# Aligned buffers, the norm's deviation moved into the residual addition, and a new order of operations

## The chip, the cores and the metric

The kernel runs on one core of a Trainium2 chip. The metric is the device time of one execution in microseconds (us). A core has five engines that run their own instruction queues side by side: TensorE (PE; its weight loads are shown as PEld), VectorE (DVE), ScalarE (ACT), GpSimd (POOL) and SyncE (SP), which issues the loads and stores here. They wait for each other by semaphores.

## What is computed

Three layers, one behind the other, in float32, on 2 batches of 768 positions and 512 channels (8 heads of 64).

```python
# 1. attention: each query sees keys within 16 positions, and 24 block summaries (max of k, mean of v)
scores = concat(where(|i - j| < 16, q k^T / 8, -1e9), q k_sum^T / 8 + log(32))
x = softmax(scores) @ concat(v, v_sum)
# 2. a gated MLP with a 3-tap convolution over positions
h = max(x @ w_in, 0)                      # 512 -> 1024
x = (h * sigmoid(conv3(h, conv_w))) @ w_out
# 3. layer norm, feed-forward, residual
xn = (x - mean(x)) / sqrt(var(x) + 1e-6) * g_ln
out = x + max(xn @ w_ch1, 0) @ w_ch2      # 512 -> 2048 -> 512
```

## The kernel before

Products that need more than one pass split an operand into a high part (rounded to fp32r) and a low part (the rest), and sum three matmuls (high x high, high x low, low x high).

Attention works on 12 blocks of 128 positions: transposes of k and q (L374, L367), scores (L479 mask, L487), softmax on VectorE, ScalarE and GpSimd, transposes of the probabilities (L586) and the product with v (L503). The MLP works on 5 groups of 2 or 3 blocks; in each it goes over 8 hidden blocks (`m_step`, numbers 0 to 39): the product with w_in (L741), relu on ScalarE (L753), three taps (L771), tanh (L776), the gate on VectorE (L786), its high part (L265/L267) and low part (L804), and the product with w_out (L818). The result, x, is copied out of PSUM by ScalarE with a row sum (L827), and a second pass gives the sum of squares (L834).

The feed-forward part goes over 16 steps; step n takes a batch b and a slice i of the hidden channels, in the order (0,0), (0,1), (1,0), (1,1), (1,2), (1,3), (0,2), (0,3) and so on. A step has seven products of six matmuls each (L1288, `pr`), a Strassen-like scheme whose sums are made by VectorE (L1299), high and low parts of the relu (L1308, L1311), and six accumulations of six matmuls (L1366, `ac`). PSUM has two banks for the products, so a product waits for the sum that frees the bank of the one before last. After the last step of a run of steps of one batch the accumulated result is added to x (L1375, L1357 at the very end) and, at the end, stored.

The norm, before: from the squares `ln_stats` makes the variance on VectorE (L1068), its power of -1/2 on GpSimd (L1071, `rs`) and mean times deviation (L1073, `nb`). Then `x_ops` normalizes each block (`xn`, L1191 on ScalarE, L1194 on VectorE), TensorE transposes it (L1229, `tp`), and it is split into high and low parts. g_ln is multiplied into w_ch1.

What stands where on an engine is set by a table, `ORDER`: some 1,930 words like `31P`, the number of an operation and the letter of the engine that runs it. The kernel records each operation with the engines that it may use, and issues them in the order of the table; each engine takes its own in that order and waits where an operand is not ready.

Buffers lie on two sides of SBUF: `const`, then `x2a` and `x2b`, then the pool `m1` (weights wi and wo, the gate's buffers) and later `m2` in its place, from the left; `at` and later `p2` from the right.

## Time and profile before

| | us |
|---|---|
| median of 3 runs (lowest, highest) | 474.7 (474.35, 474.94) |
| the profiled execution | 474.33 |
| its span, first to last instruction | 472.6 |

| engine | busy us | share of the span |
|---|---|---|
| TensorE (PE) | 462.8 | 98% |
| its weight loads (PEld) | 407.4 | 86% |
| VectorE | 351.3 | 74% |
| ScalarE | 249.4 | 53% |
| GpSimd | 142.0 | 30% |

The profiled execution's time is its span and 1.7 us around it. Times in a timeline count from the span's start. A matmul's duration covers more than the step from it to the next one, since matmuls are pipelined; start minus start tells what a stretch of them takes.

### The profile page before, as it was taken

The page shows a single profiled execution, that of the slowest core. Times are in us where ns is not written, and L with a number is a line of the kernel's source. Part 1 is how long each engine was busy: PE and PEld are TensorE (multiplying, and loading weights), DVE is VectorE, ACT ScalarE, POOL GpSimd, SP SyncE. Part 2 cuts the span into 40 slices and gives each one's busy share as a digit, 9 for nine tenths or more (in the row PEclk, how much of TensorE's full clock was granted, in tenths as well). Part 3 has the DMA queues.
Part 4 walks back from the last instruction along what each step waited for, and adds up shares of the span by engine and source line. Part 5 has one row for each costly group of instructions (what it writes and reads, how often), then busy time and mean ns, then how long its engine had stood idle before and what let it go on. Part 6 is the DMA issues. An engine that isn't in the chain of part 4 may idle for free.

```text
span 472.6 us, 8644 instructions
## 1 busy us (share of the span) xinstructions
PE 462.8 (98%) x3211; PEld 407.4 (86%) x3211; DVE 351.3 (74%) x705; ACT 249.4 (53%) x654; POOL 142.0 (30%) x185
## 2 busy tenths in 40 slices
PE   6999999999999999999999999999999999999997
PEld 5658999888899989988989899989898898998985
DVE  2899999996777857998999874677655677654643
ACT  2788999666766666958953532232343235322010
POOL 3537432554125244231513321131131331002000
PEclk9999999999999999999999999999999999999999
DMA  8999975902002202002221041201222022110213
GB/s 244 328 245 216 248 213 147 177 3 63 1 18 47 92 2 89 1 0 90 90 90 56 33 135 58 77 23 67 89 90 89 2 89 84 46 50 1 96 39 133
DMA packets 56121, 43.26 MB, mean 92 GB/s; under 512 B 34404, under 2 KB 46976, under 8 KB 56080
## 3 DMA queue, kind: packets, MB, share of 16 engines
q1 hardware_dynamic: 55936, 42.65, 32.2%
q8 instruction: 25, 0.41, 0.4%
q14 instruction: 16, 0.13, 0.1%
q10 hardware_dynamic: 144, 0.07, 0.1%
HBM read 39.22 MB, written 3.15 MB: 90 GB/s over the span
## 4 chain that ended last, share of the span: by engine, by line
PE 89%; DMA 4%; DVE 2%; SPq 2%; issue 1%; ACT 1%; POOL 1%; ACTq 0%; POOLq 0%
PE acc L1366 26%; PE ch L1288 23%; PE x L818 12%; PE h L741 6%; PE tr L741 5%; PE ch L741 4%; PE h L818 2%; PE tr L503 2%; PE tr L487 2%; PE tr L586 2%; DMA vw<-in_v_dram 2%; DMA raw<-in_moe_w_ch_dram 1%; DMA early<-in_q_dram 1%; PE acc L1229 1%; PE tr L367 1%; PE tr L479 1%
## 5 line engine op out<-in xcount | busy, mean ns | idle before, releaser
L1366 PE MATMUL acc<-w,cb 128*128 128x512 f32 x570 | 139.0, 391 | 0.0
L1366 PEld LDWEIGHTS acc<-w,cb 128*128 128x128 f32 x570 | 106.3, 188 | 19.2
L1288 PE MATMUL ch<-xb,w 128*128 128x384 f32 x384 | 75.6, 338 | 0.3 <-DVE u L1299 0.3
L1288 PEld LDWEIGHTS ch<-xb,w 128*128 128x128 f32 x384 | 68.0, 188 | 3.4 <-DVE u L1299 1.1
L1299 DVE TENSOR_TENSOR u<-ch,u 128x384 f32<-128x384 f32 x64 | 35.0, 553 | 31.1 <-PE ch L1288 30.5
L1288 PE MATMUL ch<-xt,w 128*128 128x384 f32 x288 | 56.9, 337 | 0.3 <-DVE u L1299 0.2
L771 DVE SCALAR_TENSOR_TENSOR c<-h,ccol,c 128x256 f32<-128x256 f32 (+1 forms) x80 | 48.2, 613 | 9.6 <-POOL c L269 4.9
L1288 PEld LDWEIGHTS ch<-xt,w 128*128 128x128 f32 x288 | 51.0, 188 | 2.9 <-DVE u L1299 0.9
L818 PE MATMUL x<-wo,ghi 128*128 128x512 f32 x160 | 51.5, 403 | 0.0
L1099 POOL TENSOR_TENSOR w<-raw,w 128x512 fp32r<-128x512 f32 (+1 forms) x16 | 20.5, 1282 | 82.4 <-ACT w L1166 75.4
L1308 ACT ACTIVATE cb<-p 128x384 fp32r<-128x384 f32 x32 | 16.6, 521 | 40.9 <-PE acc L1366 23.8
L557 ACT ACTIVATE prob<-tr,nm 128x120 f32<-128x120 f32 x96 | 33.2, 367 | 5.9 <-DVE nm L545 3.9
L647 ACT ACTIVATE raw<-raw 128x512 f32<-128x512 f32 x32 | 21.0, 674 | 26.2 <-DMA raw<-in_moe_w_ch_dram 24.6
L741 PE MATMUL h<-xT,wi 128*128 128x258 f32 x216 | 31.9, 288 | 0.0
L818 PE MATMUL x<-wo,glo 128*128 128x512 f32 x80 | 31.6, 394 | 0.0
L818 PEld LDWEIGHTS x<-wo,ghi 128*128 128x128 f32 x160 | 27.9, 189 | 3.4 <-ACT wo L265 0.2
L1308 ACT ACTIVATE cb<-u 128x384 fp32r<-128x384 f32 x32 | 16.1, 520 | 27.6 <-DVE u L1299 27.6
L741 PEld LDWEIGHTS h<-xT,wi 128*128 128x128 f32 x216 | 29.1, 189 | 1.7 <-ACT h L753 0.2
L741 PE MATMUL tr<-xT,wi 128*128 128x386 f32 (+1 forms) x168 | 29.3, 317 | 0.0
L741 PEld LDWEIGHTS tr<-xT,wi 128*128 128x128 f32 x168 | 26.7, 190 | 1.3 <-issue 0.4
L652 DVE SCALAR_TENSOR_TENSOR raw<-raw 128x512 uint32<-128x512 uint32 x32 | 22.9, 728 | 0.6 <-ACT raw L647 0.2
L786 DVE SCALAR_TENSOR_TENSOR gbuf<-c,h 128x256 f32<-128x256 f32 (+1 forms) x40 | 19.3, 488 | 5.1 <-ACT c L776 4.9
(192 smaller groups left out, 827.1 us busy)
## 6 DMA issues: line engine op xcount, KB each, us to landing
raw<-in_moe_w_ch_dram SPq DMA_DIRECT2D x32, 512.0 KB, 3.6
wst<-in_moe_w_out_dram SPq DMA_DIRECT2D x8, 512.0 KB, 5.8
vw<-in_v_dram SPq DMA_DIRECT2D x20, 192.0 KB, 4.8
wst<-in_moe_w_in_dram SPq DMA_DIRECT2D x5, 512.0 KB, 8.7
s_q<-in_q_dram SPq DMA_DIRECT2D x8, 256.0 KB
early<-in_k_dram SPq DMA_DIRECT2D x6, 256.0 KB, 4.3
x2a<-in_moe_w_in_dram SPq DMA_DIRECT2D x3, 512.0 KB
early<-in_v_dram SPq DMA_DIRECT2D x3, 512.0 KB
```

The costliest lines, as they stand in the source:

```text
L557: A.activation(out=pr[:, p, :], in_=sc[:, p * NK:(p + 1) * NK], func=AF.Exp, bias=nm[:, p:p + 1], scale=1.0, accum_out=sm[:, p:p + 1])
L647: A.activation(out=f, in_=f, func=AF.Prelu, scale=F64_SCALE, alpha=F64_SIGN)
L652: V.scalar_tensor_tensor(out=most, in0=most, scalar=3, in1=least, op0=ALU.logical_shift_left, op1=ALU.bitwise_or)
L741: T.matmul(live["h", i][:, 0:N + 2], w_[:, c, f * 128:(f + 1) * 128], x_[:, c, 0:N + 2], start=(k_ == 0 and c == 0), stop=(k_ == 2 and c = ...
L771: V.scalar_tensor_tensor(out=ct, in0=ht[:, kk:kk + N], scalar=ccol[:, kk * NF + f:kk * NF + f + 1], in1=ct, op0=ALU.mult, op1=ALU.add)
L786: V.scalar_tensor_tensor(out=gt, in0=ct, scalar=1.0, in1=ht, op0=ALU.add, op1=ALU.mult)
L818: T.matmul(x2ps[g, t], l[:, ts_], r[:, f, :], start=(f == 0 and j == 0), stop=(f == NF - 1 and j == 2))
L1099: lambda e: on[e].tensor_tensor(out=hi()[1], in0=from_(), in1=hi()[0].bitcast(F32), op=ALU.subtract),
L1288: T.matmul(bk[k], l[:, c, :], x_[:, c, :], start=j == 0 and c == 0, stop=j == 2 and c == 1)
L1299: lambda e: V.tensor_tensor(out=temp(to), in0=bk[k], in1=temp(x), op=ALU.add), after,
L1308: A.activation(out=half(0, r, y), in_=temp(src), func=AF.Relu)
L1366: T.matmul(acc[key], ct_[n][l][:, r, 128 * t:128 * t + 128], w2[s][k][:, r], start=first and j == 0, stop=done and j == 5)
```

## The change

Three things change.

The buffer `junk` is allocated 32 bytes longer. What comes behind it on the left side of SBUF moves by 32 bytes: `x2a`, `x2b`, the weights and, later, the operands of batch 1 and the accumulations' input begin at multiples of 64 bytes, where they began 32 past one. Behind three buffers of 1,544 bytes the gate's `ghi` and `glo` and the taps' `c` move from multiples of 64 to 32 past one. The right side stays.

`xn` becomes x minus its mean; the deviation, 1/sqrt(var), is multiplied into the residual addition, which turns from an addition of two operands into multiply-and-add with a factor per row. `nb` is gone. `xn` waits for the mean (`MN`) of its own block, and no longer for the power; the residual addition waits for the power. This rests on relu(s z) = s relu(z) for s > 0.

The table `ORDER` is another list. Its matmuls are the same in number, and 166 operations are given to another engine. A line of each:

```diff
-13S 12S 15S 14S 67S 9S 8G 3G 4G 5G 6G 68V 58V 0V 31P 32A 59A 69A 16S 11S 18S 17S 20S 73S 91S 19S 21S 39P 27P 34P 41V
...
+13S 0V 5G 9S 6G 12S 16S 11S 14S 67S 15S 3G 58V 17S 4G 31P 18S 163G 20S 73S 79S 19S 21S 10S 85S 27P 33V 91S 22S 32A 23S
...
```

The rest of the diff:

```diff
@@ -243,7 +243,7 @@
     ind = const.tile([128, 40], F32, name="ind")
     mneg = const.tile([128, B, NT], F32, name="mneg")
     ssq = const.tile([128, B, NT], F32, name="ssq")
-    junk = const.tile([128, DM], BF16, name="junk")
+    junk = const.tile([128, DM + 16], BF16, name="junk")[:, 0:DM]
     gbuf = m1.tile([128, 7 * 384], F32, name="gbuf")
     kw = [at.tile([128, 4, NW, NK], F32, name=f"kw{i}") for i in range(3)]
     qb = [at.tile([128, 4, NW, 64], F32, name=f"qb{i}") for i in range(2)]
@@ -718,7 +718,7 @@
         return [GL[u] for u in range(24 - GS[0], 24) if 256 * (u % GS[0]) < 384 * k_ + 384 and 384 * k_ < 256 * (u % GS[0]) + 256]
 
     stats_a = [(b, t) for b in range(B) for t in range(NT)]
-    SQ = {}
+    SQ, MN = {}, {}
 
     def m_step(i):
         g, f = divmod(i, NF)
@@ -835,6 +835,7 @@
                                      accum_out=ssq[:, b, i_:i_ + 1])
                     X2E[q_] = plan.op(f"xa{q_}", (("A", 700),), fe, [prev])
                     o = plan.op(f"mn{q_}", (("V", 70), ("A", 180)), fm, [X2E[q_]])
+                    MN[b, i_] = o
                     SQ[b, i_] = plan.op(f"sq{q_}", (("A", 700),), fs, [o])
                 else:
                     def fe(e, q_=q_, t=t):
@@ -1069,9 +1070,7 @@
         r = plan.op(f"va{b}", (("V", 70),), f_rs, [SQ[b, t] for t in range(NT)])
         r = plan.op(f"rs{b}", (("G", 1287),),
                     lambda e: G.tensor_tensor(out=rs[:, :, 1], in0=rs[:, :, 0], in1=mhalf, op=ALU.pow), [r])
-        r = plan.op(f"nb{b}", (("V", 70),),
-                    lambda e: V.tensor_tensor(out=rs[:, :, 0], in0=mneg[:, b, :], in1=rs[:, :, 1], op=ALU.mult), [r])
-        LNR[b] = (mneg, rs, r)
+        LNR[b] = (rs, r)
 
     ln_stats(0)
 
@@ -1176,7 +1175,6 @@
                  xt[b, j][:, 2], xb[b, 1, j][:, 2:4])[k] for j in range(2)]
 
     def x_ops(b, gate, way):
-        mv, rs, r = LNR[b]
         XF.update({(b, k): [] for k in range(7)})
         for p in range(3):
             cell = {}
@@ -1189,11 +1187,11 @@
                     i = p + 3 * h
                     if e == "A":
                         A.activation(out=cell["xn"][:, h, :], in_=x2(b * NT + i), func=AF.Identity,
-                                     bias=rs[:, i, 0:1], scale=rs[:, i, 1:2])
+                                     bias=mneg[:, b, i:i + 1], scale=1.0)
                         return
-                    V.tensor_scalar(out=cell["xn"][:, h, :], in0=x2(b * NT + i), scalar1=mv[:, b, i:i + 1],
-                                    scalar2=rs[:, i, 1:2], op0=ALU.add, op1=ALU.mult)
-                xo.append(plan.op(f"xn{b}{p}{h}", (("V", 456), ("A", 600)), f_x, [r] + gate + xo[:1],
+                    V.tensor_scalar(out=cell["xn"][:, h, :], in0=x2(b * NT + i), scalar1=mneg[:, b, i:i + 1],
+                                    scalar2=None, op0=ALU.add)
+                xo.append(plan.op(f"xn{b}{p}{h}", (("V", 456), ("A", 600)), f_x, [MN[b, p + 3 * h]] + gate + xo[:1],
                                   take=[("xn", (b, p))] if h == 0 else []))
             XO_.setdefault(b, []).extend(xo)
 
@@ -1354,7 +1352,8 @@
 
                     def f_r(e, c=c, k0=k0, k1=k1):
                         res = x2(b * NT + t)[:, k0:k1]
-                        V.tensor_tensor(out=res, in0=live["end", c], in1=res, op=ALU.add)
+                        V.scalar_tensor_tensor(out=res, in0=live["end", c], scalar=LNR[b][0][:, t, 1:2], in1=res,
+                                               op0=ALU.mult, op1=ALU.add)
                         (nc.sync, nc.scalar)[c % 2].dma_start(out=out[b, t * 128:(t + 1) * 128, k0:k1], in_=res)
                     plan.op(f"rz{n:02d}{c}", (("V", 420),), f_r, [p_] + RES[b, t])
                 continue
@@ -1372,10 +1371,11 @@
             if done:
                 def f_r(e, t=t, key=key):
                     res = x2(b * NT + t)
-                    V.tensor_tensor(out=res, in0=acc[key], in1=res, op=ALU.add)
+                    V.scalar_tensor_tensor(out=res, in0=acc[key], scalar=LNR[b][0][:, t, 1:2], in1=res,
+                                           op0=ALU.mult, op1=ALU.add)
                     if i == NP - 1:
                         nc.sync.dma_start(out=out[b, t * 128:(t + 1) * 128, :], in_=res)
-                r_ = plan.op(f"re{n:02d}{t}", (("V", 602),), f_r, [p_] + XO_[b] + RES.get((b, t), []))
+                r_ = plan.op(f"re{n:02d}{t}", (("V", 602),), f_r, [p_, LNR[b][1]] + XO_[b] + RES.get((b, t), []))
                 r_.give.append((f"acc{y}", key))
                 RES[b, t] = [r_]
```

At the start of the program GpSimd's queue before, from its first own operation on (`ident` is the identity for transposes, `mask_l` and `mask_r` the two factors of the attention mask):

```order
L333 MEMSET mhalf 128x6
L336 MEMSET kw_96 128x4x16
masks.py:197 MEMSET ident 128x128
masks.py:199 ISA
masks.py:199 AFFINE_SELECT ident<-ident 128x128
L299 MEMSET ind 128x40
L300 AFFINE_SELECT ind<-ind 128x40
L302 AFFINE_SELECT ind<-ind 128x40
L308 MEMSET mask_l 64x128
L309 AFFINE_SELECT mask_l<-mask_l 64x128
```

and of the changed kernel:

```order
L318 MEMSET mask_r 67x360
L320 AFFINE_SELECT mask_r<-mask_r 64x3x96
L322 AFFINE_SELECT mask_r<-mask_r 64x3x96
L324 MEMSET mask_r 64x16
L325 MEMSET mask_r 64x16
L327 MEMSET mask_r 3x3x24
L329 AFFINE_SELECT mask_r<-mask_r 3x3x24 x2
masks.py:197 MEMSET ident 128x128
masks.py:199 AFFINE_SELECT ident<-ident 128x128
```

Both masks, seven operations of `mask_r` and three of `mask_l` ahead of the rows shown, now stand ahead of the identity.

Where step 0 of the feed-forward part begins, VectorE's queue before (`p`, `u` are the temporaries of the products' sums, `w` the high and low parts of the weights, `ch` a product in PSUM, `mneg` the mean):

```order
L1099 TENSOR_TENSOR xb_2471<-sg,xb_2470 128x4x128
L269 TENSOR_SCALAR mneg<-mneg 128x1 x3
L267 COPY p_3019<-ch 128x384
L1099 TENSOR_TENSOR w_3006<-raw,w_3005 128x512 x2
L1299 TENSOR_TENSOR u_3035<-ch,p_3019 128x384
L1299 TENSOR_TENSOR u_3040<-ch,u_3035 128x384
L1068 TENSOR_SCALAR rs<-ssq 128x6
L1299 TENSOR_TENSOR p_3058<-ch,u_3040 128x384
L1299 TENSOR_TENSOR u_3035<-ch,u_3035 128x384
L1299 TENSOR_TENSOR p_3019<-ch,p_3019 128x384
```

and of the changed kernel (line numbers are two lower there from the norm on, one lower for the low parts):

```order
L269 TENSOR_SCALAR mneg<-mneg 128x1
L1098 TENSOR_TENSOR xt_2464<-ts,xt_2463 128x6x128
L1098 TENSOR_TENSOR w_3004<-raw,w_3003 128x512
L269 TENSOR_SCALAR mneg<-mneg 128x1
L1297 TENSOR_TENSOR u_3028<-ch,p_3015 128x384
L1297 TENSOR_TENSOR u_3042<-ch,u_3028 128x384
L1297 TENSOR_TENSOR u_3028<-ch,u_3028 128x384
L1297 TENSOR_TENSOR p_3057<-ch,u_3042 128x384
L1192 TENSOR_SCALAR xn<-x2b,mneg 128x512
L1297 TENSOR_TENSOR p_3015<-ch,p_3015 128x384
```

Of the low-part copies of the weights one has left the stretch and a low-part copy of the transposed input (`xt`) has come into it; the first copy out of PSUM and the two operations on `rs` are gone from it.

On ScalarE at the same place, before:

```order
L827 ACTIVATE x2b,mneg<-h 128x512
L1166 CAST w_3005<-raw 128x512 x2
L834 ACTIVATE junk,ssq<-x2b,mneg 128x512 x3
L647 ACTIVATE raw<-raw 128x512
L1308 ACTIVATE cb_3071<-p_3019 128x384
L1191 ACTIVATE xn<-x2b,rs 128x512
L1118 ACTIVATE raw<-raw,ccol 128x256 x2
```

and of the changed kernel:

```order
L827 ACTIVATE x2b,mneg<-h 128x512
L1165 CAST w_3003<-raw 128x512
L265 COPY p_3015<-ch 128x384
L265 ACTIVATE mneg<-mneg 128x1
L1165 CAST w_3003<-raw 128x512
L834 ACTIVATE junk,ssq<-x2b,mneg 128x512 x2
L1189 ACTIVATE xn<-x2b,mneg 128x512
L834 ACTIVATE junk,ssq<-x2b,mneg 128x512 x2
```

The subtraction (`xn`) stands behind two squares (`junk,ssq`) of the last three blocks and two are left behind it; the first copy out of PSUM (`p<-ch`) has come in.

On TensorE the products of step 0 stand in the same order; the transposes of batch 1 (L1229, L1227 now) come behind six products, where seven stood ahead of them. Between the last product of the MLP with w_in (L741) and the first use of its hidden block stood 17 uses of other hidden blocks (three matmuls of L818 each) and eight transposes; now 12 and four.

## Rows read from the trace of the kernel before

**Rows 1.** The page, part 1: busy time, share of the span, instructions.
```profile
PE 462.8 (98%) x3211; PEld 407.4 (86%) x3211; DVE 351.3 (74%) x705; ACT 249.4 (53%) x654; POOL 142.0 (30%) x185
```

**Rows 2.** Waits of TensorE: who waited for whom; us in total, times, longest.
```profile
PE tr L374 <- POOL mask_r L320: 3.9, 1, 3.9
PE tr L374 <- DMA early<-in_q_dram: 0.7, 1, 0.7
...
PE tr L586 <- DVE prob L576: 0.4, 1, 0.4
PE acc L1229 <- ACT raw L1118: 0.4, 1, 0.4
PE tr L374 <- DMA early<-in_k_dram: 0.2, 1, 0.2
```

**Rows 3.** Timeline of GpSimd, 0 to 12 us: start, duration, engine, line, operation.
```profile
0.91 0.20 POOL masks.py:197 MEMSET ident<- 128x128 f32 x1
1.19 0.29 POOL masks.py:199 TENSOR_SCALAR_AFFINE_SELECT ident<-ident 128x128 f32<-128x128 f32 x1
...
2.08 0.20 POOL L308 MEMSET mask_l<- 64x128 bf16 x1
...
4.80 0.56 POOL L329 TENSOR_SCALAR_AFFINE_SELECT mask_r<-mask_r 3x72 bf16<-3x72 bf16 x2
```

**Rows 4.** Timeline of TensorE at 214 us, where the products of step 0 begin.
```profile
213.97 1.23 PE L1288 MATMUL ch<-xb,w 128*128 128x384 f32 x6
215.03 1.20 PE L1288 MATMUL ch<-xt,w 128*128 128x384 f32 x6
...
217.52 1.33 PE L1288 MATMUL ch<-xt,w 128*128 128x384 f32 x6 [0.24 <-DVE u L1299]
...
219.96 1.31 PE L1288 MATMUL ch<-xt,w 128*128 128x384 f32 x6
...
222.70 1.07 PE L1229 MATMUL acc<-ident,xn 128*128 128x128 f32 x8 [0.39 <-ACT raw L1118]
```

**Rows 5.** Timeline of VectorE at the same place.
```profile
215.71 1.29 DVE L1099 TENSOR_TENSOR w<-raw,w 128x512 fp32r<-128x512 f32 x2
216.91 0.55 DVE L1299 TENSOR_TENSOR u<-ch,p 128x384 f32<-128x384 f32 x1
```

**Rows 6.** Timeline of ScalarE at the same place.
```profile
220.96 0.81 ACT L1191 ACTIVATE xn<-x2b,rs 128x512 f32<-128x512 f32 x1
```

**Rows 7.** Timeline of GpSimd at the same place.
```profile
218.66 1.34 POOL L1071 TENSOR_TENSOR rs<-rs,mhalf 128x6 f32<-128x6 f32 x1 [5.22 <-DVE rs L1068]
```

**Rows 8.** Timeline of VectorE at 186 us: the gate and a tap.
```profile
185.57 0.55 DVE L786 SCALAR_TENSOR_TENSOR gbuf<-c,h 128x384 f32<-128x384 f32 x1
186.04 0.60 DVE L771 SCALAR_TENSOR_TENSOR c<-h,ccol,c 128x384 f32<-128x384 f32 x1
```

**Rows 9.** Groups of VectorE by line and shape: count, busy us, mean ns, idle before.
```profile
L1299 DVE TENSOR_TENSOR u<-ch,u 128x384 f32<-128x384 f32 x64 | 35.0, 553 | 31.1 <-PE ch L1288 30.5
L771 DVE SCALAR_TENSOR_TENSOR c<-h,ccol,c 128x384 f32<-128x384 f32 x32 | 24.5, 772 | 5.6 <-ACT c L265 3.5 <-POOL c L269 1.8
...
L1375 DVE TENSOR_TENSOR x2a<-acc,x2a 128x512 f32<-128x512 f32 x18 | 12.0, 684 | 6.6 <-PE acc L1366 6.6
```

**Rows 10.** Line 1288, 254 to 265 us (step 3): ns min/median/max, first and last start.
```profile
L1288 PE MATMUL ch<-xb,w x27: 333/334/340, 253.6 to 264.4; 128*128 128x384 f32 x27
```

**Rows 11.** Line 1288, 301 to 313 us (step 6).
```profile
L1288 PE MATMUL ch<-xb,w x27: 334/335/346, 300.5 to 312.6; 128*128 128x384 f32 x27
```

**Rows 12.** Line 1288, 316 to 330 us (step 7).
```profile
L1288 PE MATMUL ch<-xb,w x24: 336/339/341, 316.5 to 329.2; 128*128 128x384 f32 x24
```

**Rows 13.** Timeline of ScalarE: relu of the last hidden block.
```profile
199.25 0.49 ACT L753 ACTIVATE h<-ch 128x386 f32<-128x386 f32 x1 [0.44 <-PE ch L741]
```

**Rows 14.** Timeline of TensorE: first uses of the last hidden block.
```profile
211.86 0.63 PE L818 MATMUL x<-wo,ghi 128*128 128x512 f32 x2
...
212.56 0.63 PE L818 MATMUL x<-wo,ghi 128*128 128x512 f32 x2
```

More of the change, by code (lines that the diff above doesn't have):

```diff
@@ new lines @@
+1158V 1171P 1257V 1170P 1161V 1260P 1159V 1164A 1243V 1177A 1160V 1165G 1262P 1261V 1166A 1163V 1267P 1258A 1167G
+1264V 1263V 1265A 1279P 1225A 1268V 1178V 1219A 1218V 1172A 1271P 1220V 1173V 1278P 1221A 1174V 1259V 1222G 1175V
+1281P 1272V 1181A 1176V 1224V 1269A 1280P 1345S 1282A 1226V 1179A 1182V 1227A 1285P 1273A 1270V 1283P 1228V 1274V
+1350S 1304P 1266V 1347A 1284V 1286V 1306P 1180V 1287A 1289P 1352A 1310P 1290V 1346V 1351V 1348V 1291P 1288V 1349G
+1312P 1293V 1292V 1294A 1305V 1300P 1295V 1353V 1296P 1301V 1354A 1314P 1297V 1302A 1360A 1303V 1298A 1308P 1355V
@@ new lines @@
+1359A 1357V 1299V 1363G 1313V 1316P 1356G 1311V 1318P 1317A 1358G 1396S 1324P 1362A 1319V 1069V 1364V 1366G 1326P
+1325V 1401S 1307V 1342P 1327V 1398A 1328V 1309V 1320P 1331P 1321V 1315V 1322A 1335P 1361A 1397V 1403A 1399V 1344P
+1400V 1332V 1410A 1340P 1329A 1365V 1414G 1323V 1343P 1402V 1330V 1336V 1341P 1404V 1405V 1367P 1406V 1408V 1407G
+1339P 1412A 1337A 1418S 1368A 1338V 1333A 1369P 1409V 1411A 1334V 1371P 1415V 1370V 1424S 1393P 1372V 1373A 1375P
+1391P 1376V 1419V 1426A 1425V 1420A 1382P 1427V 1421V 1377P 1392P 1379V 1383V 1380A 1422A 1395P 1384A 1423G 1413A
@@ new lines @@
+1428A 1390P 1417V 1416G 1436S 1378V 1394P 1374V 1429G 1442P 1386P 1443V 1430S 1444P 1387V 1385V 1388A 1450P 1438A
+1389V 1437V 1466P 1445V 1439V 1451V 1446P 1452P 1447V 1381V 1448A 1461P 1432A 1454V 1453V 1440A 1467P 1462V 1455A
+1441G 1449V 1457P 1535S 1431V 1471P 1433V 1458V 1470P 1434A 1472A 1463A 1473P 1464V 1435V 1537A 1479P 1459A 1474V
+1540S 1460V 1469P 1480V 1456V 1536V 1468P 1541V 1542A 1481P 1543V 1475P 1538V 1544A 1483V 1465P 1539G 1482V 1476V
+1502P 1070G 1545V 1490P 1486P 1491V 1547V 1496P 1487V 1549A 1477A 1546V 1553G 1488A 1478V 1504P 1550A 1586S 1484A
@@ new lines @@
+1554G 1551A 1506P 1505V 1492A 1555G 1489V 1498P 1507A 1548V 1508P 1588A 1493V 1591S 1587V 1510P 1509V 1503V 1500P
+1485V 1511V 1514P 1494P 1515V 1497V 1501V 1557P 1512A 1589V 1552A 1529P 1513V 1590A 1558V 1556V 1516P 1499V 1525P
+1517V 1518V 1532P 1495V 1519A 1593A 1592V 1526V 1521P 1594V 1520V 1595A 1531P 1522V 1523A 1596V 1601A 1559P 1527A
+1605G 1600A 1528V 1530P 1597G 1598V 1534P 1604G 1560V 1524V 1585P 1599G 1608S 1614S 1533P 1565P 1610A 1580P 1566V
+1602A 1609V 1611V 1567P 1616A 1581P 1568V 1569V 1615V 1572P 1617V 1618A 1583P 1573V 1603A 1612A 1607V 1576P 1561P
@@ L96 @@
+1877V 1890P 1911P 1891V 1882P 1896P 1883V 1892A 1901P 1898V 1899A 1914P 1902V 1893V 1903A 1897V 1912P 1904V 1905P
+1920P 1906V 1907A 1913P 1908V 1900V 1909P 1918P 1922P 1919V 1916P 1923V 1924P 1917V 1915V 1928P 1921V 1926P 1925V
+1929V 1927V
 """
```

159 lines of the change are left out of this document (68 added, 91 removed).

## The prediction

> **What bounds the kernel now.** I read the page's busy times first: TensorE is busy for 462.8 us, 98% of the span [rows 1]. So only three things can move the time: how long one matmul takes, the stretches in which TensorE is not fed, and what lies ahead of its first and behind its last matmul. Next I read the list of TensorE's waits [rows 2]: one of 3.9 us ahead of the first transpose, and after it only 0.2, 0.7, 0.4 and 0.4 us. The page understates such losses, since a matmul that starts late shows as a late start and not as idle time. So third, where the feed-forward part begins, I took start minus start from the timeline [rows 4]. A product of six matmuls takes 1.06 us there undisturbed (213.97 to 215.03). The next two take 2.49 us, the two after them 2.44, and the two up to the transposes 2.74. Beyond 1.06 us each, 0.37, 0.32 and 0.62 us are lost: 1.31 us at one place, and the largest loss that I found between the first matmul and the last.
>
> **The change, part by part.** Both programs hold the same matmuls in the same number; what is left is order, addresses and a few small operations.
>
> *The start.* GpSimd now builds the two masks before the identity matrix that the first transposes need. Before, the identity was ready at 1.48 us and the masks ran from 2.08 to 5.36 [rows 3], 3.28 us of work. Put first, at about 0.85 us, the masks end at about 4.15; the identity takes 0.57 us (0.91 to 1.48), so it is ready at about 4.7. The first transpose began after 3.9 us [rows 2]; the identity had then been ready for 2.4 us, so the wait that is put down to GpSimd was for the first load of k. Now the identity is the later of the two, by some 0.8 us. What hides this: TensorE went on to wait 0.2 us for k and 0.7 us for q [rows 2], and the q load that it needs is ninth in the queue where it was tenth, so a later start meets data that have landed. Those two waits hold 0.9 us. If they cover all, the cost is 0; if the cover is gone, 0.8. I take +0.2, nearer to full cover.
>
> *The start of the feed-forward part.* Two things go. First, VectorE's queue: the second partial sum (L1299, 216.91) stood behind two low-part copies of the output weights that took 1.29 us together from 215.71 [rows 5]. In the new order one of the two is GpSimd's and the first copy out of PSUM is ScalarE's; the sum then comes some 0.65 us earlier, and the 0.37 us behind it goes. Second, the wait of the normalized input for the deviation. The normalization of batch 1 began at 220.96 and took 0.81 us [rows 6], behind all six squares and behind GpSimd's power, 1.34 us from 218.66 [rows 7], with one small VectorE operation on either side of that. Now the subtraction waits for the mean alone, and in ScalarE's new order it stands behind two squares. Without the power it would begin by 220.96 - 1.34 = 219.6 and end by 220.4 at the latest, and TensorE, with six products ahead of the transposes in place of seven, comes to them at 213.97 + 6 x 1.06 = 220.3. So of the 0.62 us the wait for the input, some 0.5, goes. Of the 0.32 us in the middle I count 0.2, since VectorE still makes the same five sums in a row. Together 0.37 + 0.5 + 0.2 = 1.07, taken as -1.1. The bounds: all of it, -1.3; or, because a third low-part copy (of the transposed input, on GpSimd before) now also stands ahead of the sums on VectorE and costs half as much again as one of the two in [rows 5], about 0.97 us, the queue is as late as it was and only the 0.5 goes.
>
> *The deviation in the residual.* Thirty additions (18 for batch 0, 684 ns on average [rows 9], 12 for batch 1) and the two last ones turn from a plain addition into multiply-and-add with a per-row factor. A three-operand instruction with such a factor took 0.60 us for 384 columns, with a constant in its place 0.55 [rows 8]; so I add 0.05 to 0.06 us each. For those inside, the cover is VectorE's own waiting for TensorE ahead of them, 6.6 us for the 18 [rows 9]; without it they would cost 1.8 us. The last one lies on the path: +0.05. The subtraction of the mean loses a factor and can only get shorter, and the two operations that made mean times deviation go, both off TensorE's path but for the gain counted above. The additions now wait for the power, and GpSimd runs that of batch 1 late, behind a scaling of weights that waits for a load. Two products and two accumulations stand between it and the first addition that needs it, 2.1 us for the products alone [rows 4] against its 1.34 [rows 7], so I take the wait as empty; were it not, the sums of the next step would queue behind that addition on VectorE, and TensorE's next products wait for those.
>
> *The addresses.* By the built programs' addresses the weights, the accumulated input and the feed-forward operands of batch 1 began 32 bytes past a multiple of 64 and now begin on one; the operands of batch 0 were on one already, and the gate's high and low parts, which were on one, are moved off it. So the kernel before has each combination. Both operands 32 past: 333/334/340 ns for a 384-column matmul [rows 10]. Both on a multiple: 334/335/346 [rows 11]. Moving on, weights off: 336/339/341 [rows 12]. The new product steps are all of the second kind. At most the 168 matmuls of the third kind gain 4 ns, 0.7 us; the 288 of the gate (L818) get the third kind's combination and could lose up to 4 ns, 1.2 us. I take 0.
>
> *The rest of the list.* Of the 1,930 operations of the list some 165 change engine, three small broadcasts of sums go from the load queue to VectorE, and nearly all operations have new neighbours. Of the waits outside the two places above, 0.4 us (L586) and what shows in [rows 2] only in part can go; as many new ones can come. I take -0.4; bounds -1.2 and +1.5.
>
> **Sum.** +0.2 - 1.1 + 0.05 + 0 - 0.4 = -1.25 us. The profiled execution took 474.33 us by the clock (472.6 us of span and 1.7 around it): 473.1. It lies 0.4 below the median of the runs, 474.7, so for a median I say **473.4**.
>
> **Rivals.**
> (a) *The start is not absorbed and the list gives nothing else back*: +0.8 instead of +0.2, 0 instead of -0.4: 474.7 - 0.25 = 474.4, no change. For it: a load of weights and two of k have changed places in the queue, so the 0.2 and 0.7 us need not recur. Against it: the first five groups of transposes still run ahead of the q that the sixth waits for.
> (b) *The tail of the first MLP becomes a wait* (slower). The last hidden block's relu began at 199.25 [rows 13] and its first use on TensorE at 211.86; one use takes 0.70 (to 212.56) [rows 14]. Cover: 12.6 us. In the new order five such uses and half of the transposes have moved ahead of that block, so the cover is 12.6 - 5 x 0.70 - 0.4 = 8.7. The chain is eight instructions of about 0.55 us [rows 8], some 4.4 us undisturbed, but spread over the queues it took up to 12.6 before. If it again takes over 10.9 us (8.7 plus the 1.25 gained plus 0.95), the kernel is slower; at the old pace it loses 3.9 us: 477.3. Against it: fewer of these blocks' copies are GpSimd's in the new list.
> (c) *Blocking between VectorE and GpSimd lands elsewhere.* The 384-column multiply-add took 772 ns on average [rows 9] against 0.60 in [rows 8], so others wait inside: 0.17 x 32 = 5.5 us of VectorE time. The list gives GpSimd 151 operations instead of 159; if a tenth of that time came back on the path, -0.5 more: 472.9; if it lands on the sums (L1299), for which a product waits directly, +0.5 to +1.5: 474 to 475.
> The Trainium skill ("SBUF — State Buffer", section "SBUF: two separate sides") says that a VectorE operation with two SBUF inputs and a GpSimd operation that reads SBUF take a shared port pair by turns, the loser blocked for the whole instruction. By that rule the sums at L1299, with one operand in PSUM, are never blocked, and the slower half of (c) falls; the trace agrees as far as means go, 553 ns for those sums against 772 [rows 9].
> (d) *Addresses matter more than I say, or the list clears most waits*: -0.7 and -1.2 instead of 0 and -0.4: 471.9.
>
> **Chances.** The forecast 0.42 (472.6 to 474.2); (a) 0.22; (b) 0.11; (c) 0.11, even on both sides; (d) 0.14. To leave out no more than 2 in 10 the range takes in (a), (c) and (d) and the near end of (b): 471.9 to 475.8. A measurement here can tell about 0.2% (0.95 us) from no change, that is below 473.75 or above 475.65. Faster: (d), half of (c) and three fifths to two thirds of the forecast, but some of (a) as well: 0.50. Slower: (b) and a part of (c): 0.16. Same: 0.34.
>
> **What would show it.** In the profile after: a first transpose at about 4.7 us and no wait for q behind it (start); from the first product to the first transpose six products in under 6.9 us, where seven took 8.73 (the feed-forward start); the residual additions at 0.72 to 0.75 us (deviation); 384-column matmuls at 334 to 336 ns throughout (addresses). I am wrong if the start of the first block of the MLP is later than before, if TensorE waits for the gate's low part near 210 us, or if matmul durations change by more than 1%.

## The result: 477.1 us, slower by half a per cent

| | before | changed |
|---|---|---|
| median of 4 runs (lowest, highest), us | 474.52 (474.35, 474.94) | 477.12 (476.86, 478.18) |
| profiled execution, us | 474.33 | 476.86 |
| its span, us | 472.6 | 475.0 |

The ratio is 1.0051, 95% interval 1.0035 to 1.0067. The forecast was 473.4, its range ended at 475.8: wrong in sign.

### The profile page after: what moved, and what is told of

Its sections match the earlier page's. It is cut to its first block, busy times and chain, and to the rows that moved or that the text cites. A ratio compares the mean times of both kernels' runs of the same rounds, so it can differ in the third digit from the quotient of the medians.

```text
span 475.0 us, 8628 instructions
## 1 busy us (share of the span) xinstructions
PE 463.3 (98%) x3211; PEld 407.1 (86%) x3211; DVE 360.4 (76%) x710; ACT 248.6 (52%) x655; POOL 138.0 (29%) x180
## 4 chain that ended last, share of the span: by engine, by line
PE 89%; DVE 5%; DMA 3%; ACT 1%; issue 1%; SPq 1%; POOL 0%; POOLq 0%
PE acc L1365 27%; PE ch L1286 23%; PE x L818 11%; PE tr L741 5%; PE h L741 5%; PE ch L741 4%; PE h L818 2%; PE tr L503 2%; PE tr L487 2%; PE tr L586 2%; DMA vw<-in_v_dram 2%; DMA wst<-in_moe_w_in_dram 1%; PE tr L479 1%; PE tr L367 1%; PE tr L374 1%
## 5 line engine op out<-in xcount | busy, mean ns | idle before, releaser
L1365 PE MATMUL acc<-w,cb 128*128 128x512 f32 x570 | 140.8, 392 | 0.0
L1286 PE MATMUL ch<-xb,w 128*128 128x384 f32 x384 | 76.7, 337 | 0.4 <-ACT w L1143 0.4
L1286 PEld LDWEIGHTS ch<-xb,w 128*128 128x128 f32 x384 | 68.0, 188 | 3.7 <-ACT w L1143 0.7
L1297 DVE TENSOR_TENSOR u<-ch,u 128x384 f32<-128x384 f32 x64 | 35.2, 553 | 32.8 <-PE ch L1286 31.9
L1286 PE MATMUL ch<-xt,w 128*128 128x384 f32 x288 | 57.7, 336 | 0.7 <-DVE u L1297 0.6
L1286 PEld LDWEIGHTS ch<-xt,w 128*128 128x128 f32 x288 | 51.0, 188 | 3.5 <-DVE u L1297 0.9
L818 PE MATMUL x<-wo,ghi 128*128 128x512 f32 x160 | 51.3, 401 | 0.0
L771 DVE SCALAR_TENSOR_TENSOR c<-h,ccol,c 128x256 f32<-128x256 f32 (+1 forms) x80 | 44.9, 575 | 6.1 <-POOL c L269 4.0
L1098 POOL TENSOR_TENSOR w<-raw,w 128x512 fp32r<-128x512 f32 (+1 forms) x16 | 19.3, 1208 | 93.6 <-ACT w L1165 61.5
L741 PE MATMUL h<-xT,wi 128*128 128x258 f32 x216 | 32.0, 288 | 0.1
L818 PE MATMUL x<-wo,glo 128*128 128x512 f32 x80 | 31.6, 395 | 0.0
L741 PEld LDWEIGHTS h<-xT,wi 128*128 128x128 f32 x216 | 29.3, 190 | 2.4 <-DVE xT L267 0.4
L818 PEld LDWEIGHTS x<-wo,ghi 128*128 128x128 f32 x160 | 28.0, 189 | 3.6
L741 PE MATMUL tr<-xT,wi 128*128 128x386 f32 (+1 forms) x168 | 28.9, 319 | 0.3 <-DVE ksum L395 0.3
L1119 POOL TENSOR_SCALAR raw<-raw,ccol 128x256 f32<-128x256 f32 x8 | 7.7, 982 | 67.5 <-DVE raw L652 67.5
L741 PEld LDWEIGHTS tr<-xT,wi 128*128 128x128 f32 x168 | 26.4, 190 | 1.1 <-issue 0.5
L1309 DVE SCALAR_TENSOR_TENSOR cb<-u,cb 128x384 fp32r<-128x384 f32 x32 | 19.3, 602 | 6.5 <-ACT cb L1306 6.4
```

The costliest lines, as they stand in the source:

```text
L741: T.matmul(live["h", i][:, 0:N + 2], w_[:, c, f * 128:(f + 1) * 128], x_[:, c, 0:N + 2], start=(k_ == 0 and c == 0), stop=(k_ == 2 and c = ...
L771: V.scalar_tensor_tensor(out=ct, in0=ht[:, kk:kk + N], scalar=ccol[:, kk * NF + f:kk * NF + f + 1], in1=ct, op0=ALU.mult, op1=ALU.add)
L818: T.matmul(x2ps[g, t], l[:, ts_], r[:, f, :], start=(f == 0 and j == 0), stop=(f == NF - 1 and j == 2))
L1098: lambda e: on[e].tensor_tensor(out=hi()[1], in0=from_(), in1=hi()[0].bitcast(F32), op=ALU.subtract),
L1286: T.matmul(bk[k], l[:, c, :], x_[:, c, :], start=j == 0 and c == 0, stop=j == 2 and c == 1)
L1297: lambda e: V.tensor_tensor(out=temp(to), in0=bk[k], in1=temp(x), op=ALU.add), after,
```

## The profile after

The page, part 1, of the changed kernel, answers to [rows 1], and its list of TensorE's waits to [rows 2]:

```profile
PE 463.3 (98%) x3211; PEld 407.1 (86%) x3211; DVE 360.4 (76%) x710; ACT 248.6 (52%) x655; POOL 138.0 (29%) x180
```

```profile
PE tr L374 <- POOL ident masks.py:199: 4.8, 1, 4.8
PE ch L1286 <- DVE u L1297: 0.6, 1, 0.6
PE tr L503 <- DMA vw<-in_v_dram: 0.6, 2, 0.3
PE x L374 <- ACT kw L265: 0.5, 1, 0.5
PE ch L1286 <- ACT w L1143: 0.4, 1, 0.4
PE tr L503 <- DVE wst L643: 0.4, 1, 0.4
PE tr L741 <- DVE ksum L395: 0.3, 1, 0.3
```

The waits for q and k are gone, as the prediction had it, and six others have come. VectorE is busy 9 us longer. To see where the time went, cut the span at three starts that both traces have: the first hidden product (first matmul of L741), the first feed-forward product (first of L1288, now L1286) and the last matmul.

| us | before | changed | difference |
|---|---|---|---|
| start to first hidden product | 43.40 | 43.96 | +0.56 |
| from there to the first feed-forward product | 170.57 | 171.90 | +1.33 |
| from there to the last matmul's start | 254.79 | 255.21 | +0.42 |
| from there to the end | 3.87 | 3.90 | +0.03 |

Of the first two, one group of transposes (0.45 us) has only moved from the first part to the second.

**First MLP.** Inside the 1.33 us two places stand out. The first two rows are VectorE's, the third TensorE's; then two of VectorE and one of the weight loads:

```profile
58.16 0.68 DVE L652 SCALAR_TENSOR_TENSOR wst<-wst 128x512 uint32<-128x512 uint32 x1
58.85 0.66 DVE L395 TENSOR_REDUCE ksum<-tr 128x16 f32<-128x512 f32 x1
...
59.65 0.72 PE L741 MATMUL tr<-xT,wi 128*128 128x258 f32 x4 [0.33 <-DVE ksum L395]
...
62.30 0.67 DVE L395 TENSOR_REDUCE ksum<-tr 128x16 f32<-128x512 f32 x1
62.91 0.67 DVE L267 COPY probT<-tr 120x512 f32<-120x512 f32 x1
...
63.65 0.66 PEld L503 LDWEIGHTS tr<-probT,vw 120*64 120x64 f32 x19 [0.25 <-ACT c L776]
```

At 59.65 TensorE wants a bank of PSUM that a window maximum on VectorE (`kmb40`, L395) has still to read; that stood behind a step of narrowing weights (L652). Start minus start, 0.49 us are lost. At 63.65 the product with v needs the copy of the transposed probabilities (`C8`, L267) that VectorE ended at 63.58: 0.34 us. The profile names ScalarE there, whose operation had ended before; the copy is the operand that came last.

VectorE came late to the first of these as follows. Four microseconds earlier a gate operation took 1.55 us. It had begun 0.04 us behind a low part on GpSimd (VectorE, then GpSimd):

```profile
54.79 1.55 DVE L786 SCALAR_TENSOR_TENSOR gbuf<-c,h 128x256 f32<-128x256 f32 x1
...
54.75 1.31 POOL L664 TENSOR_TENSOR wi<-x2a,wi 128x512 fp32r<-128x512 f32 x1 [5.53 <-ACT wi L265]
```

From there to `kmb40` VectorE had no pause: with a gate of 0.4 us the maximum could have begun up to 1.1 us earlier, more than the 0.49 us lost.

**Start of the feed-forward part.** TensorE, answering to [rows 4], and VectorE ahead of the last of these rows:

```profile
215.86 1.20 PE L1286 MATMUL ch<-xb,w 128*128 128x384 f32 x6
...
221.34 1.33 PE L1286 MATMUL ch<-xt,w 128*128 128x384 f32 x6
222.50 1.04 PE L1227 MATMUL acc<-ident,xn 128*128 128x128 f32 x8
...
225.03 1.32 PE L1286 MATMUL ch<-xb,w 128*128 128x384 f32 x6 [0.42 <-ACT w L1143]
...
237.60 1.14 PE L1286 MATMUL ch<-xt,w 128*128 128x384 f32 x5 [0.58 <-DVE u L1297]
```

```profile
235.53 0.41 DVE L1246 TENSOR_TENSOR sg<-sg 128x256 f32<-128x256 f32 x1
235.86 0.42 DVE L1246 TENSOR_TENSOR ts<-sg,ts 128x256 f32<-128x256 f32 x1
236.20 0.55 DVE L1309 SCALAR_TENSOR_TENSOR cb<-p,cb 128x384 fp32r<-128x384 f32 x1
236.66 0.41 DVE L1246 TENSOR_TENSOR ts<-acc,ts 128x256 f32<-128x256 f32 x1
237.00 0.55 DVE L1297 TENSOR_TENSOR u<-ch,u 128x384 f32<-128x384 f32 x1
```

Six products take 222.50 - 215.86 = 6.64 us. Then 0.68 us are lost at 225.03, where the first product of the next step waits for its weights, and 0.85 at 237.60 (0.58 and 0.75 at the start, 0.1 behind it in each), where a product waits for a bank that a sum (`pd01`, L1297) frees only at 237.55, since four other operations stood ahead of it.

## Experiments

In the diffs the words of the list carry the operation's name in place of its number, so `kmb40V` is that maximum on VectorE; "old" is the list of before, "new" that of the changed kernel, and "old" lists run with the new norm. Ratios are to the kernel before, run beside it (medians of before 474.7 to 475.1). The three columns are the stretches of the table above, from one profiled execution each.

| run | to hidden | MLP | feed-forward | ratio (95%) |
|---|---|---|---|---|
| before | 43.40 | 170.57 | 254.79 | |
| changed | 43.96 | 171.90 | 255.21 | 1.0051 (1.0035, 1.0067) |
| e1 addresses alone | 43.88 | 170.61 | 255.24 | 1.0010 (0.9994, 1.0025) |
| e2 norm alone | 43.44 | 170.57 | 255.12 | 0.9996 (0.9984, 1.0008) |
| e4 new, from first hidden on old | 43.90 | 170.58 | 254.94 | 1.0000 (0.9985, 1.0016) |
| e5 old, from first product on new | 44.31 | 171.13 | 255.70 | 1.0025 (1.0010, 1.0040) |
| e10 old to step 3, then new | 44.21 | 170.60 | 254.37 | 0.9988 (0.9978, 0.9999) |
| e7 v loads first | 50.71 | 171.89 | 255.67 | 1.0198 (1.0185, 1.0211) |
| e9 two max moves | 43.63 | 171.85 | 255.69 | 1.0063 (1.0042, 1.0084) |
| e8 two VectorE moves | 43.36 | 171.86 | 256.70 | 1.0053 (1.0041, 1.0065) |
| e12 e8, no GpSimd beside | 42.73 | 171.86 | 255.54 | 1.0038 (1.0022, 1.0053) |
| e13 both mended | 43.09 | 172.32 | 256.12 | 1.0039 (1.0026, 1.0053) |
| e14 e10 mended | 43.88 | 170.62 | 254.20 | 0.9985 (0.9970, 1.0001) |
| e15 old engines at two places | 43.80 | 171.02 | 256.39 | 1.0038 (1.0025, 1.0050) |
| e17 new order, old engines | 43.78 | 174.88 | 256.43 | 1.0123 (1.0109, 1.0136) |
| e18 old order, new engines | 48.85 | 178.56 | 255.56 | 1.0299 (1.0286, 1.0313) |
| e19 two places old | 43.99 | 171.01 | 254.72 | 0.9999 (0.9983, 1.0016) |
| e20 two places mended | 43.30 | 171.07 | 254.78 | 0.9987 (0.9968, 1.0006) |

The column to the hidden product scatters by 0.9 us between executions of one list (43.40 to 44.31 for the six that begin with the old one), the MLP column by 0.05 except in e5 (0.55 longer, 0.3 of it at one group of transposes at 66.3 us). The feed-forward column scatters too: changed, e5, e7 and e9 have the same words there, and the last three took 255.67 to 255.70 us against 255.21. So the profiled execution of before had the shortest start of its kind, and that of changed the shortest feed-forward part.

### One part alone

**e1**: `-junk = const.tile([128, DM], ...)`, `+junk = const.tile([128, DM + 16], ...)[:, 0:DM]` in the kernel before. **e2**: the norm's part of the diff in the kernel before, `nb0V` and `nb1V` taken out of its list.

> The kernel before, with its list and its norm, and the scratch buffer widened by 16 columns: only the addresses change. Theory A (the list costs the time, addresses cost nothing): 474.5 us, within 0.5, and 384-column matmuls of 334 to 337 ns as before. Rival B (the new addresses cost the time, by transfers or by VectorE): 476 to 477 us. Rival C (the addresses save what rival (d) of the prediction gave them): 473.8 us.

> The kernel before, with its list and its addresses, and the deviation in the residual addition (the two operations that made mean times deviation gone from the list, everything else in its place). Theory A (the list costs the time): 474.0 to 474.8 us; of the 0.55 us that TensorE lost ahead of the transposes at 222.7 us up to 0.5 may go, since the normalization no longer waits for the power. Rival D (the edit itself costs the time, by longer residual additions and by additions that wait for the power): 476 to 477 us, with the loss inside the feed-forward steps.

Neither costs what the change costs. In e1 the products' matmuls take 334 ns in the median, and the MLP takes as long as before; its interval does not tell 0 from 0.2%. In e2 the additions got longer as predicted (groups of VectorE by line and shape, answering to [rows 9]):

```profile
L1374 DVE SCALAR_TENSOR_TENSOR x2a<-acc,rs,x2a 128x512 f32<-128x512 f32 x18 | 13.1, 745 | 6.5 <-PE acc L1365 6.5
```

and the time did not. Nor did the normalization come earlier. ScalarE's and TensorE's rows of e2:

```profile
219.78 0.68 ACT L647 ACTIVATE raw<-raw 128x512 f32<-128x512 f32 x1 [1.36 <-DMA raw<-in_moe_w_ch_dram]
220.56 0.53 ACT L1306 ACTIVATE cb<-p 128x384 fp32r<-128x384 f32 x1
220.99 0.71 ACT L1189 ACTIVATE xn<-x2b,mneg 128x512 f32<-128x512 f32 x1
```

It starts at 220.99, as in [rows 6], though it no longer waits for the power: a narrowing of the next weights stood ahead of it, waiting for their load. The power was not what held it.

### Which part of the list

```diff
 e4   ORDER = new up to h0a (first hidden product), then what is left of old
 e5   ORDER = old up to pr000 (first feed-forward product), then what is left of new
 e10  ORDER = old up to pr030 (first product of step 3), then what is left of new
```

> The changed kernel with its list up to the first product of the first MLP; all other operations behind it in the order and on the engines of the list before. Theory A with the loss split as the two traces show it: the first product comes 0.6 us later than before with 0.5 us less work behind it, so 475.4 to 475.7 us. Rival E (everything is lost behind, at the start of the feed-forward part): 474.5 us.

> The changed kernel with the list before up to the first product of the feed-forward part, and its own list behind. By the two traces the new list loses 0.7 us more than the old one between 214 and 250 us and gets 0.45 back later, so theory A expects 474.7 to 475.0 us. Rival E (the feed-forward start carries the whole loss): 476.5 to 477 us.

> The changed kernel with the list before up to the first product of step 3 of the feed-forward part (about 240 us), and its own list behind. Theory A (the new list is worse up to 240 us and better behind, where the old one loses 0.29 us at 369 and 0.56 us at 391): 473.6 to 473.9 us, faster than both kernels by 0.8 us or more. Rival K (the two late losses of the old list depend on what lies ahead and come back): 474.5.

The new start costs nothing; the new list from the first product on costs 0.25%; with the old list up to step 3 and the new one behind the kernel is a little faster than before. So the loss lies in what the old list does between 44 and 255 us. By their times e5 lies between its two theories, and e10's 474.5 us is rival K's number, though the two late losses that K counted on are not in its trace.

### The attention's loads

e7, on the load queue (S):

```diff
-lw7S lq2S ... lv1S ... lv0S ... lw8S ... lv2S
+lq2S lv1S lv0S lv2S lw7S ... lw8S
```

> The changed kernel with one edit: on the load queue the q chunk and the three first window loads of v stand ahead of the weight loads lw7 and lw8. Theory A (in the attention part TensorE, earlier than before at 37 us, runs into loads of v that land late): the three losses at 36.4, 39.6 and 40.6 us (0.43, 0.55, 0.54 us in the changed kernel) go or shrink, and the time falls by 0.5 to 1.2 us, to 476.0 to 476.6. Rival F (TensorE waits there for VectorE and ScalarE, not for loads): the three losses stay, 477.1. Rival G (the two weight loads are then late for the hidden layer's weights): as many new waits behind 44 us, 477 to 478.

```profile
38.22 0.43 DVE L643 TENSOR_SCALAR wst<-wst 128x512 uint32<-128x512 uint32 x1 [7.93 <-DMA wst<-in_moe_w_in_dram]
...
41.89 0.91 PE L503 MATMUL tr<-probT,vw 120*64 120x64 f32 x12 [6.10 <-DVE vw L636]
```

VectorE waited 7.9 us for the weights of lw7, whose narrowing stands early in its queue, and the rows of vsum and everything else behind it waited too. That is rival G with another victim than it named, and it leaves F undecided. e16 (`lv2S` alone ahead of `lw8S`, in a list of new start, e14's middle and new end) gave 1.0011 (0.9998, 1.0023), no gain over e14, so its theory A falls; where it lost time is not read from its trace.

> New list to the first hidden block, with the third window load of v ahead of the weight load lw8; then the mended old list to step 3 of the feed-forward part; then the new list. Theory A (the start of the new list is 0.6 us shorter, and only the late loads of v hide it): the losses at 39.6 and 40.6 us shrink, and the time is 473.5 to 474.0 us, below both kernels. Rival F (the loads are as late wherever this one stands): 474.4 to 474.8, as the mended old list alone.

### The place in the first MLP

```diff
 e9   -wo10cV R8V kmb40V ... wo11zV wo10eG kmb41V
      +kmb40V wo10cV R8V ... kmb41V b5A wo11zV wo10eG
 e11  as e9, and  -wo11zV ... P8P ... C8V   +kmb41V P8P C8V wo11zV
 e15  -b0V u0A qe31A v0V kn41V kn40A u2A C8V   (order as it was)
      +b0G u0G qe31V v0G kn41A kn40V u2G C8A
```

> The changed kernel with two words moved on VectorE in the first MLP: the two window maxima of chunk 4 (kmb40, kmb41) ahead of a step of narrowing that they stood behind. Theory A (the losses of 0.49 and 0.34 us at 59.6 and 63.7 us come from VectorE reading a bank of PSUM late): both go, 476.3 us. Rival J (the next copy on VectorE is then late): 477.1.

> The changed kernel with the two maxima of chunk 4 ahead of the narrowing steps, as in the run with the two max moves, and in addition the copy C8 of the transposed probabilities ahead of the narrowing wo11z (that run lost 0.91 us at 63.3 us, with C8 standing behind that narrowing). Theory A (VectorE's order alone makes the two losses of 0.49 and 0.34 us at 59.6 and 63.7 us): both go, 0.8 us less than the changed kernel: 476.3 us. Rival J (VectorE is short of time in that stretch, whatever its order): the loss of some 0.8 us stays, 477.1.

In e9 the loss at 59.6 went, and came back at 63.3 (VectorE, GpSimd, VectorE, TensorE):

```profile
57.37 1.63 DVE L652 SCALAR_TENSOR_TENSOR wst<-wst 128x512 uint32<-128x512 uint32 x1
...
57.14 1.31 POOL L664 TENSOR_TENSOR wo<-wst,wo 128x512 fp32r<-128x512 f32 x1 [1.12 <-ACT wo L265]
...
61.09 0.67 DVE L395 TENSOR_REDUCE ksum<-tr 128x16 f32<-128x512 f32 x1
61.69 0.93 DVE L643 TENSOR_SCALAR wst<-wst 128x512 uint32<-128x512 uint32 x1
62.54 0.68 DVE L267 COPY probT<-tr 120x512 f32<-120x512 f32 x1
...
63.32 0.88 PE L503 MATMUL tr<-probT,vw 120*64 120x64 f32 x23 [0.71 <-ACT wst L647]
```

C8 was now the last in the row. But the moves also met GpSimd: the narrowing L652, put behind the maximum, took 1.63 us where it takes 0.68 in the changed kernel, since it began 0.23 us behind a GpSimd operation, and L643 took 0.93 for 0.41 beside the next one. With C8 ahead as well (e11: 1.0049) the time stayed; e13, which has these moves and e12's, shows the MLP at 172.32, the loss at other products, and L652 at 1.72 us. So these runs show that the moves gain nothing, and leave open whether VectorE is short of time there.

> The changed kernel with the moves of both runs above (C8 and the maxima in the first MLP; the two VectorE moves and ys11 on VectorE in the feed-forward part). Theory A: the two gains add, 475.3 to 475.7 us. Rival J and M: 477.0 to 477.8.

What did help are letters (e15). VectorE's share in the windows of before, changed and e15:

```profile
43.40:64.00 20.60, 20.60 (x232) 18.78 (x231) 19.52 (x43) 18.89 (x63) 10.53 (x15) 1.00 1.03 236
```
```profile
44.00:66.00 22.00, 21.53 (x236) 19.72 (x237) 21.38 (x44) 19.32 (x66) 9.33 (x12) 1.00 0.99 231
```
```profile
44.00:66.00 22.00, 22.00 (x242) 20.30 (x242) 21.38 (x43) 19.76 (x65) 12.68 (x16) 1.00 0.96 228
```

(Columns: window, its length, then busy time of TensorE, its loads, VectorE, ScalarE, GpSimd, each with its count; granted clock.) Changed, VectorE is busy 21.38 of 22.0 us, TensorE 21.53. In e15, with eight operations back on the engines of before, TensorE is busy all 22.0 us and the MLP takes 171.02: 0.88 less. That is 170.57 and the 0.45 of moved transposes. VectorE's busy time is the same 21.38 us in both, so a full VectorE alone does not tell the two apart. The gate does, here in e15 (VectorE, then GpSimd):

```profile
54.73 0.42 DVE L786 SCALAR_TENSOR_TENSOR gbuf<-c,h 128x256 f32<-128x256 f32 x1
...
55.32 1.32 POOL L664 TENSOR_TENSOR wi<-x2a,wi 128x512 fp32r<-128x512 f32 x1 [3.18 <-ACT wi L265]
```

GpSimd comes later, the gate takes 0.42 us, and nothing is lost at either product. So it is in the other executions with these words: 1.55 to 1.57 us and some 0.5 lost in changed, e7, e8 and e12, 0.42 and nothing in e15, e19 and e20. That the eight letters make the loss is shown; that they make its first part, 0.49 us, by this blocking is read from rows, as no run moved GpSimd's operation alone. The time of e15, 476.9, is Q's all the same, by its other nine letters.

> The changed kernel with its own order, and 17 operations back on the engines of the list before: 8 between the first hidden block and the pair of value products at 63 us, 9 between the first product and step 3 of the feed-forward part. Theory P (the choice of engines overloads VectorE or puts GpSimd beside it at these two places): the losses of 0.83 and 0.8 us go, 475.3 to 475.7 us. Rival Q (the order makes them): 476.9 to 477.5.

### The place at the feed-forward start

```diff
 e8   -pg00V tp100P rs00A wac10V        +wac10V pg00V tp100P rs00A
      -tb11V os00V td11V pr014P pd01V   +pd01V tb11V os00V td11V pr014P
 e12  as e8, and  -ys11G ... yp11V      +yp11V ys11V
```

> The changed kernel with two words of the list moved on VectorE at the start of the feed-forward part: the third narrowing of the second weight block ahead of a sum that waits for TensorE (wac10 before pg00), and the sum pd01 ahead of two transform subtractions and a low-part copy. Theory A (two new waits of 0.58 and 0.75 us, plus 0.1 each behind them, at 225.0 and 237.6 us come from VectorE's order): both go, 475.6 to 476.1 us. Rival H (the load behind the second weight block is what is late): the first stays, only 0.85 goes, 476.3. Rival I (what is gained is lost again within a few products): 477.1.

> The kernel with the two VectorE moves, and in addition the low part ys11 taken from GpSimd to VectorE behind the next low part. In that run a multiply-add os00 took 1.65 us while GpSimd computed ys11 (1.31 us from 0.08 us earlier), and TensorE lost 1.64 us behind it at 238.7 us. Theory L (the two block each other): os00 takes 0.55 us, the loss at 238.7 falls to 0.3 to 0.6 us, and the time to 476.2 to 476.6 us. Rival M (VectorE's work in this stretch is the bound, whoever is beside it): the added 0.68 us on VectorE eat the gain, 477.3 to 477.8.

e8's wait for pd01 went, and a longer one came behind it (VectorE, GpSimd, TensorE):

```profile
235.99 1.65 DVE L1309 SCALAR_TENSOR_TENSOR cb<-p,cb 128x384 fp32r<-128x384 f32 x1
...
235.91 1.31 POOL L1098 TENSOR_TENSOR xb<-sg,xb 128x512 fp32r<-128x512 f32 x1 [1.51 <-ACT xb L1261]
...
238.71 1.17 PE L1365 MATMUL acc<-w,cb 128*128 128x512 f32 x4 [1.48 <-DVE xb L1098]
```

A multiply-add that takes 0.55 us took 1.65: it began 0.08 us behind a GpSimd operation and ended 0.42 behind its end. With that operation off GpSimd (e12) it took 0.55 again and the loss fell from 1.64 to 0.53 us, but 0.53 came at 240.1, and the feed-forward part was no shorter than in the changed kernel. L is right about the blocking, M about the time. The nine letters of e15 in this stretch made the part 1.2 us longer: 1.0 us is lost there at the product with the next weights (0.68 at 225.03 above) and 0.54 at 243.3. Here, other than in the MLP, giving the letters back did not remove the loss.

One more place costs time in this part, though not in the profiled execution of changed. The new list has the variance of batch 1 (L1069, 0.16 us) at 262 us, beside a low part on GpSimd. In e9 (VectorE, then GpSimd):

```profile
262.02 1.29 DVE L1069 TENSOR_SCALAR rs<-ssq 128x6 f32<-128x6 f32 x1
...
262.00 1.29 POOL L1098 TENSOR_TENSOR w<-ss,w 128x512 fp32r<-128x512 f32 x1 [0.73 <-ACT w L1146]
```

The sums behind it come late, and TensorE loses 0.33 us at 266.0. e5 shows the same; in e7 the next VectorE operation was blocked instead (1.79 us for 0.68). In changed VectorE began first, GpSimd's operation took 1.74 us, and TensorE lost nothing: of the 0.46 to 0.49 us by which these executions differ, 0.3 is this.

**e14** takes the two things that the prediction counted on to e10:

```diff
-wo00V ... wab10A waz10V rp00A wac10V pr006P xn100A pg00V wg10A xn101V
+wo00G ... xn100A wab10A xn101V waz10V rp00A wac10V pr006P pg00V wg10A
```

> The kernel with the old list to step 3, with the two things alone that the prediction counted on at the feed-forward start: the second low-part copy of the output weights on GpSimd, so that the first sum comes 0.6 us earlier, and the two normalizations xn100 and xn101 ahead of the narrowing that waits for a load. Theory A (the two terms are right, and were lost in the changed kernel to other places of the list): the losses of 0.51 at 218.3 and 0.47 at 223.4 us go, 0.9 us less than that kernel's 474.5: 473.5 to 473.8 us. Rival N (the weights of the next block are the limit there, by their load): the gain comes back as a wait at the first product of the next block, 474.5.

SyncE, ScalarE and TensorE of e14:

```profile
216.94 1.56 SPq L1090 DMA_DIRECT2D raw<-in_moe_w_ch_dram  x2
...
220.29 0.68 ACT L647 ACTIVATE raw<-raw 128x512 f32<-128x512 f32 x1 [0.78 <-DMA raw<-in_moe_w_ch_dram]
222.06 0.96 ACT L1117 ACTIVATE raw<-raw,ccol 128x256 f32<-128x256 f32 x2 [0.68 <-DVE raw L652]
223.06 0.43 ACT L1143 CAST w<-raw 128x256 fp32r<-128x256 f32 x1
...
222.28 1.03 PE L1227 MATMUL acc<-ident,xn 128*128 128x128 f32 x8
223.55 1.31 PE L1286 MATMUL ch<-xb,w 128*128 128x384 f32 x6 [0.23 <-ACT w L1143]
```

Both losses go: the transposes start with no wait. But 0.58 us come back at 223.55, at the first product with the next weights, and 0.14 more at a product ahead. Those weights are loaded into a buffer that is free only when the low part of the output weights has been made; load (3.3 us), narrowing and cast take 6.6 us from there. Of 0.98 us won, 0.17 stay. N is right.

### Order against engines, and the two places alone

```diff
 e17  order of new, all 166 letters of old        e18  order of old, all 166 letters of new
 e19  new, but e15's eight letters in the MLP, and old (order and letters) from pr000 to pr030
 e20  as e19, and e14's moves
```

> The changed kernel with its own order and all 166 operations back on the engines of the list before. Theory P (the choice of engines makes the loss): 475.0 to 475.7 us. Rival Q (the order makes it): 477 us or more, since order and engines were chosen together.

> The changed kernel with the order of the list before and the 166 operations on the engines of the new list. Theory P (the choice of engines makes the loss): 476.0 to 477.0 us. Rival Q (the order makes it): 474.5 to 475.2.

> The changed kernel with its own list but for two places: the 8 letters back in the first MLP, and from the first product of the feed-forward part to step 3 order and engines of the list before. Theory A (the two places hold the whole loss, 0.85 and 0.8 us in the traces, and the rest of the list is as good or better): 474.3 to 475.0 us. Rival S (a part is spread over the rest): 475.5 us or more.

> As the run with two places old, and the second low-part copy of the output weights on GpSimd and the two normalizations ahead of the narrowing that waits for a load. Theory A: 0.1 to 0.3 us less than that run, since the wait comes back at the first product with the next block of weights. Rival (it does not come back here): 0.9 us less.

Either half with the other's partner is far slower than both lists (1.0123, 1.0299): P falls with both runs, Q with e18. Order and engines only work together. With the two places as before and the rest new, the kernel is as fast as before (0.9999): the two hold the loss, the second with the variance, which e19 has at 220 us again. Versions a little faster than the kernel before are e10 and, not told apart from that kernel, e14 and e20, by 0.1 to 0.15%.

## Why the prediction was wrong, point by point

- **The rest of the list** (-0.4, bounds -1.2 and +1.5): the step that failed in sign. It was a guess over places that were not looked at. The new list puts two copies, a tap and a low part on VectorE at a place where it was busy 19.5 of 20.6 us already, as a windows view of before shows, and takes two copies off; with it GpSimd's low part comes to stand beside a gate. It cost 0.88 us. Its late part did bring something: behind step 3 the old list loses 0.9 us at two products in the execution before, the new one nothing there (e10), but in e5, e7 and e9 it loses 0.3 at 266 us.
- **The feed-forward start** (-1.1): right as far as it was worked out. Six products took 6.64 us (under 6.9 was the mark), so 1.03 us were won. What failed is that the sum stopped there: "where a stall goes" was not followed to the next product with new weights and the next full queue. 0.68, 0.85 and 0.23 us (234.26, transposes) came behind, and the stretch to 250 us lost 0.8 us more than before. That the power held the normalization was wrong: e2 takes the power away and nothing moves. The order did it.
- **The start** (+0.2): the first transpose came at 4.85 us, as said, and the cover held. The first scores began at 16.78 us, against 17.02 before. e4 gives 1.0000.
- **The deviation** (+0.05): 744 ns against 684, within the 0.72 to 0.75 named; e2 gives 0.9996.
- **The addresses** (0): the median of the products' matmuls fell from 336 to 334 ns and no stretch got shorter (e1). The changed kernel's rows, to [rows 10 to 12]:

```profile
L1286 PE MATMUL ch<-xb,w x384: 333/334/440, 215.9 to 459.8; 128*128 128x384 f32 x192
```

- **Rival (b)** named 477.3, next to what was measured, and did not happen. Its cover came out as worked out (213.76 - 205.09 = 8.67 us for 8.7), but the chain took 7.98 and TensorE did not wait (ScalarE, VectorE, TensorE of the changed kernel):

```profile
205.09 0.50 ACT L753 ACTIVATE h<-ch 128x386 f32<-128x386 f32 x1 [1.27 <-PE ch L741]
...
212.51 0.56 DVE L804 TENSOR_TENSOR glo<-gbuf,ghi 128x384 fp32r<-128x384 f32 x1 [0.24 <-ACT ghi L265]
...
213.76 0.63 PE L818 MATMUL x<-wo,ghi 128*128 128x512 f32 x2
```

- **Rival (c)**, the blocking, came true by another road than it named, and with 0.11, even on both sides, it was given too little. Its slower half was let fall because the sums are not blocked, and they are not: 0.55 us in both kernels. But other operations are, and what stands behind them in VectorE's queue is late: the maximum in the first MLP (0.49 us), the sums behind the variance (0.3 us in e5, e7 and e9), and the moves of e8, e9 and e13 came to nothing in part by it. How much of the 2.5 us it makes in all, no run shows.
- **The time of before** that the sum was made against: its execution had the shortest start of the six seen with that start, 0.45 us under their mean of 43.85. Some of the 2.3 us between the two profiles is that.

What stays open: between the changed kernel and e19 the traces show 0.89 us in the MLP and 0.49 in the feed-forward part, 1.4 in all, where the ratios are 0.52% or 2.5 us apart, with some 0.2% of uncertainty on either. With the feed-forward part of e5, e7 and e9 in place of the profiled one it is 1.9. The scatter of the start may be the rest; no run shows it. Nor was it settled whether earlier loads of v would keep what the new start gains.
